# Interleaving two MLP blocks in thirds instead of halves: an attention, MLP and mixture-of-experts kernel on one core

## The chip, the cores and the metric

The kernel runs on one core of one Trainium2 chip. The metric is the device time of one execution in microseconds (us). The engines of a core are named as the profile names them: PE (TensorE, matmuls; PEld is its weight load), DVE (VectorE), ACT (ScalarE), POOL (GpSimd) and SP (SyncE, which here only issues DMAs).

## The reference

Three layers follow one another; the first two are what the change touches.

```python
def _attn_ref(q, k, v):                      # q, k, v: 4 batches x 8 heads x 576 x 64
    scores = scale * np.matmul(q, k.transpose(0, 1, 3, 2))
    mask_local = (rel >= 0) & (rel < stride)                 # heads 0-3, stride 32
    mask_strided = (rel >= 0) & (pos[None, :] % stride == pos[:, None] % stride)   # heads 4-7
    scores = np.where(masks[None, :, :, :], scores, -1000000000.0)
    ...                                      # softmax
    return np.matmul(attn, v)

def _moe_ref(x, w_gate, w_val, w_out):       # x: 2304 tokens x 512; FF = 1536
    g = x @ w_gate
    silu = g * (1.0 / (1.0 + np.exp(-g)))
    return (silu * (x @ w_val)) @ w_out

def _moe2_ref(x, ...):                       # 8 experts, each token goes to its two best
    ...                                      # router, then relu(x @ w1[e]) @ w2[e], weighted and summed
```

w_gate, w_val and w_out arrive as float64. q, k, v and the weights of the second mixture layer are float32.

## The kernel before, in words

**Tiling.** The 2304 tokens are six blocks (j = 0 to 5) of 384; the FF dimension of the MLP is twelve chunks (c = 0 to 11, `NC1`) of 128. One *chunk* below means one pair (j, c): `m_gate` (line 490) and `m_val` (line 498) make a 128x384 tile each from 12 matmuls, and `m_out` (line 513) adds the product into three PSUM banks of the block with 9 matmuls, one chunk later (`pend`). float32 operands are split into a high and a low half (`split`, line 402: a cast on ScalarE, a subtraction on VectorE or POOL), and three of the four products are taken (`PASSES`).

**VectorE's and ScalarE's part of a chunk.** ScalarE takes tanh of the gate (line 494); VectorE makes th (line 495), the product with the value tile (line 502) and its lower half (line 404, hhl); ScalarE makes the upper half (line 403). The gate and value tiles share two PSUM buffers (`ps_gv`), so the next gate's matmuls wait for line 495 or 502 of the chunk before.

**Weights.** Each 128-wide chunk of w_gate and of w_val is one *piece*. Its 512 KB of float64 are loaded into one of three `raw` buffers by a DMA on SP's queue (`load_weight`, line 408); `weight` (line 421) turns the float64 bit patterns into float32 with three VectorE operations (lines 427 to 429); `split` makes the halves, the lower one on POOL for chunk 1 and all later ones. The twelve finished chunks stay in SBUF (`W`). w_out is not kept: each chunk needs its own copy (`load_wo`, `split_wo`, lines 456 and 463). For block 0 it is loaded as float64, converted as above, split with POOL, and its float32 form written to the buffer wod in DRAM; later blocks load that, and VectorE makes the lower half.

**Attention.** It is a generator (line 354) of 56 *quads* (four heads by up to 128 queries): transposes of q and k, scores, softmax (VectorE lines 306 to 318, ScalarE line 309), transposes, product with v, all on the same engines. Its results land in `ring`. `NEED` (line 652) says how many quads each block needs: 11 for block 0, 22 for block 1, 28 for block 2, and so on.

**The order of the work around the change.** Before the MLP starts, eleven quads are done, and some matmuls on zeros keep the PE busy. Then `seq` (line 655) lists the chunks. Blocks 0 and 1 are interleaved in halves, since block 1 can use a weight chunk as soon as block 0 has used it: block 0 chunks 0 to 5, block 1 chunks 0 to 5, block 0 chunks 6 to 11, block 1 chunks 6 to 11. I call these four stretches of six chunks *runs*. Blocks 2 to 5 then follow whole. Each chunk has three `slot` calls (line 692) that advance attention towards `goal` (line 658) at a pace of 18 slots in a run of six chunks, and advance the routing of a finished block by one step. All of quads 11 to 21 stand in run 0; runs 1 and 2 have no attention (their goal is the same 22, and all six PSUM banks hold the two blocks' sums); run 3 has quads 22 to 27 and block 0's routing. At the end of each run the x halves of the next run's block are made (`split_x`, line 473; four operations on ScalarE and four on VectorE, five buffers).

In run 0 each chunk loads and makes the weights one or two chunks ahead (`load_wgv`, `split_wgv`). After run 0, `half_wgv` (line 449) makes one piece at a time and issues the load of the piece two further on; `MADE` (line 443) says how many pieces of the later chunks are made by the end of each step: with the entries below two pieces in the first step after run 0, two in the second, one in the third, and so on.

```python
MADE = (2, 4, 5, 7, 9, 10, 11, 12)
...
elif i - HC < len(MADE):
    for n in range(MADE[i - HC - 1] if i > HC else 0, MADE[i - HC]):
        half_wgv(HC + n // 2, n % 2)
```

The main loop is at line 817. `late_consts` (line 136: twelve small DMAs on SP's queue) is called at block 1's first chunk, `zero_dram` (line 146: 22 stores of zeros on SP's queue) at block 2's first. Which instruction stands where on an engine is decided when the program is built: a planner may set instructions that depend on nothing late ahead of others, so the order on an engine is not quite the order of the text.

Of the kernel before, what the change touches and what calls it, by code (L numbers as in the profile page):

```python
# [21 lines left out]
def attention_moe_kernel(ctx: ExitStack, tc: tile.TileContext, q, k, v, w_gate, w_val, w_out,  # L22
# [9 lines left out]
    NC1 = FF // P  # L32
# [11 lines left out]
    NBLK = NT // 384  # L44
# [387 lines left out]
    def load_wgv(c):  # L432
        for i, src in enumerate((w_gate, w_val)):
            load_weight(("gv", c, i), src[:, c * P:(c + 1) * P])

    def split_wgv(c):
        W[c] = wp.tile([P, 4, DM], F32R, name="W", tag="W")
        eng = nc.gpsimd if c >= 1 else None
        for i in range(2):
            split(W[c][:, 2 * i], W[c][:, 2 * i + 1], weight(("gv", c, i)), eng)  # L440


    MADE = (2, 4, 5, 7, 9, 10, 11, 12)

    def load_half(c, i):
        if c < NC1:
            load_weight(("gv", c, i), (w_gate, w_val)[i][:, c * P:(c + 1) * P])

    def half_wgv(c, i):
        if i == 0:  # L450
            W[c] = wp.tile([P, 4, DM], F32R, name="W", tag="W")
        x = weight(("gv", c, i))
        load_half(c + 1, i)
        split(W[c][:, 2 * i], W[c][:, 2 * i + 1], x, nc.gpsimd)
# [196 lines left out]

    NEED = [11, 22, 28, 39, 50, 56]

    HC = NC1 // 2
    seq = [(j, c) for h in range(2) for j in range(2) for c in range(h * HC, (h + 1) * HC)]
    seq += [(j, c) for j in range(2, NBLK) for c in range(NC1)]

    goal = [NEED[1], NEED[1], NEED[1], NEED[2]] + [NEED[min(j + 1, NBLK - 1)] for j in range(2, NBLK)]
    
    def part(i):  # L660
        return i // HC if i < 4 * HC else 2 + i // NC1

    warm = ps_gv.tile([P, DM], F32, name="warm", tag="gv")

# [27 lines left out]
    def slot(i):  # L692
        if early and had5[0] and not rts:
            next(early[0], None)
        if rts:
            if next(rts[0], "end") == "end":
                rts.pop(0)
        p = part(i)
        g0, pace = goal[p - 1] if p else NEED[0], 36 if p > 3 else 18
        nslot[0] += 1  # L700
        if goal[p] > g0:
            want = g0 + (goal[p] - g0) * min(nslot[0], pace) / pace
            while adone[0] < want - PB:
                if next(att, "end") == "end":
                    break
# [91 lines left out]
    def early_steps():  # L797
        load_info(0, 0, 4)
        load_info(1, 0, 4)
        for _ in range(EY[0]):  # L800
            yield
        info(0, 0)
        info(1, 0)
        for t in range(2):
            gather(0, t, EARLY)
            yield
        for _ in range(EY[1]):
            yield
        for t in range(4):
            xtrans(0, t)  # L810
            if t < 2:
                gather(0, t + 2, EARLY)
            for _ in range(3):
                yield

    EY = (3, 4, 2)
    for i, (j, c) in enumerate(seq):
        if j == NBLK - 1 and c == 0:
# [3 lines left out]
            early.append(early_steps())  # L822
        if i < HC:
            if c + 2 < HC:
                load_wgv(c + 2)
            if c + 1 < HC:
                split_wgv(c + 1)
            else:
                for n in range(2):
                    load_half(HC, n)  # L830
# [3 lines that stand above are left out]
# [8 lines left out]
        split_wo(i)  # L842
        m_gate(j, c)
        slot(i)
        m_val(j, c)
        if i + 1 < len(seq) and part(i + 1) > part(i):
            att_until(goal[part(i)])
            nslot[0] = 0
            for kk in KORD:
                split_x(seq[i + 1][0], kk)  # L850
        slot(i)
        if pend:
            pj, pc = pend.pop()
# [5 lines left out]
        if j == NBLK - 1 and c >= 1 and wnext[0] < E * NC2 and wnext[0] < 12:  # L859
            prep_w()  # L860
        slot(i)
        pend.append((j, c))

# [132 lines left out]
    with tc.If(worst > 0):  # L996
        for e in range(E):
            s0, nov = e * REG + CAP[e], (REG - CAP[e]) // P
            last = nc.values_load(ntile[0:1, e:e + 1], min_val=0, max_val=nov)
            with tc.For_i(0, last, 1) as t:  # L1000
# [17 lines left out]
                for c in range(NC2):  # L1018
# [8 lines left out]
                    h = ov.tile([P, P], F32, name="o_h")  # L1027
# [35 lines left out]
```

## Time and profile before

| | us |
|---|---|
| median of three runs | 1071.08 |
| lowest and highest | 1070.45, 1072.36 |
| profiled execution, its own time | 1072.54 |
| its span, first to last instruction | 1070.8 |
| chunks 0 to 5 (run 0), by the first gate matmul of each stretch | 64.4 |
| runs 1 and 2 (no attention) | 81.3 |
| run 3 | 52.2 |
| from the third block to the end of the span | 822.5 |

The profiled execution's time is 1.7 us more than its span, and 1.5 us more than the median of the three runs. Stretches are told in us from the start of the span. A busy time on VectorE includes time in which an instruction is held up by another engine's use of the memory.

### The profile page before, as it was taken

The numbers are of one execution on the slowest core, as the hardware profiler recorded it, in microseconds if no ns is written. First come the engines' busy times: TensorE is split into PE (matmuls) and PEld (weight loads), VectorE is DVE, ScalarE is ACT, GpSimd is POOL, SyncE is SP. The second block draws the span as 40 slices with busy tenths as digits, with TensorE's granted clock in tenths as the row PEclk, the third lists the DMA queues.
The fourth block names the chain that finished last, engine by engine and source line by source line (L and its number), as shares of the span: only waits on it lengthen the run. The fifth ranks groups of instructions, "written<-read, shape, count | busy, mean of one in ns | idle before, by whom it ended". The sixth has DMA issues, their size and how long they took to land. (4 is left out here: it accounts for less than half of the span.)

```text
span 1070.8 us, 17472 instructions
## 1 busy us (share of the span) xinstructions
PE 1032.2 (96%) x6262; PEld 896.1 (84%) x6268; DVE 582.1 (54%) x1528; ACT 443.5 (41%) x1107; POOL 374.9 (35%) x425
## 2 busy tenths in 40 slices
PE   7999999999999999999998989999999999999994
PEld 4677888878888888889988878999888888888884
DVE  6899897474565664453464625444545444544210
ACT  4776442454454554442453424343434333333211
POOL 6154333024031231020014527455545454545211
PEclk9999999999999999999999999999999999999997
DMA  8688465269362641221344607546554545453212
GB/s 184 152 218 201 132 185 167 67 191 199 94 78 64 137 51 55 77 63 41 99 148 96 211 1 148 119 102 156 128 126 126 128 110 141 107 146 68 36 21 30
DMA packets 186961, 123.26 MB, mean 115 GB/s; under 512 B 96224, under 2 KB 154080, under 8 KB 186864
## 3 DMA queue, kind: packets, MB, share of 16 engines
q1 hardware_dynamic: 168256, 92.23, 34.0%
q0 software_dynamic: 16016, 25.10, 12.7%
q10 hardware_dynamic: 2592, 4.72, 1.2%
q8 instruction: 51, 0.84, 0.3%
q14 instruction: 46, 0.38, 0.1%
HBM read 98.04 MB, written 23.91 MB: 114 GB/s over the span
## 5 line engine op out<-in xcount | busy, mean ns | idle before, releaser
L893 PE MATMUL acc<-W,hhl 128*128 128x512 f32 (+1 forms) x960 | 243.3, 393 | 2.8 <-DVE hhl L885 2.7
L881 PEld LDWEIGHTS ps_h<-xg,W 128*128 128x128 f32 x1536 | 229.4, 188 | 14.1 <-ACT xg L403 1.7
L881 PE MATMUL ps_h<-xg,W 128*128 128x256 f32 (+2 forms) x1536 | 239.8, 305 | 1.3 <-ACT xg L403 1.3
L893 PEld LDWEIGHTS acc<-W,hhl 128*128 128x128 f32 (+1 forms) x960 | 170.3, 184 | 36.4 <-DVE hhl L885 3.6
L751 POOL DMA_INDIRECT xrow<-x1d,idq x152 | 153.1, 1007 | 113.8 <-DVE xgT L540 57.1
L487 PE MATMUL ps_v<-xh,W 128*128 128x384 f32 x864 | 172.3, 344 | 3.3 <-DVE th L502 3.3
L487 PE MATMUL ps_g<-xh,W 128*128 128x384 f32 x864 | 169.3, 342 | 2.9 <-DVE th L495 2.4
L520 PE MATMUL acc<-wohl,hhl 128*128 128x512 f32 x648 | 169.3, 400 | 0.5 <-ACT hhl L403 0.4
L487 PEld LDWEIGHTS ps_g<-xh,W 128*128 128x128 f32 x864 | 150.2, 188 | 13.2 <-DVE th L495 4.8
L487 PEld LDWEIGHTS ps_v<-xh,W 128*128 128x128 f32 x864 | 151.5, 190 | 7.4 <-DVE th L502 3.9
L885 DVE SCALAR_TENSOR_TENSOR hhl<-ps_h,hhl 128x256 fp32r<-128x256 f32 (+2 forms) x128 | 60.2, 470 | 171.4 <-ACT hhl L884 171.4
L884 ACT ACTIVATE hhl<-ps_h 128x256 fp32r<-128x256 f32 (+2 forms) x128 | 54.7, 428 | 212.5 <-PE ps_h L881 212.4
L520 PEld LDWEIGHTS acc<-wohl,hhl 128*128 128x128 f32 x648 | 119.4, 189 | 25.2 <-issue 1.3
L404 DVE TENSOR_TENSOR W<-raw,W 128x512 fp32r<-128x512 f32 x128 | 83.8, 688 | 54.4 <-ACT W L403 52.7
L906 POOL DMA_INDIRECT out_dram<-y,ids x40 | 64.3, 1607 | 122.6 <-ACT y L905 113.1
L403 ACT CAST W<-raw 128x512 fp32r<-128x512 f32 x128 | 74.1, 618 | 64.9 <-PE acc L893 45.6
L633 POOL DMA_INDIRECT slotd<-payload,si x36 | 37.5, 1042 | 125.9 <-DVE si L620 88.4
L403 ACT CAST hhl<-th 128x384 fp32r<-128x384 f32 x72 | 36.9, 513 | 93.9 <-DVE th L502 93.8
L495 DVE SCALAR_TENSOR_TENSOR th<-th,ps_g 128x384 f32<-128x384 f32 x72 | 39.7, 551 | 57.4 <-ACT th L494 57.4
L232 POOL DMA_DIRECT2D v<-in_v_dram x28 | 19.4, 696 | 143.1 <-PE ps_o L337 129.0
L494 ACT ACTIVATE th<-ps_g 128x384 f32<-128x384 f32 x72 | 35.3, 490 | 77.0 <-PE ps_g L487 74.7
L309 ACT ACTIVATE sc<-sc,mn 126x126 f32<-126x126 f32 (+3 forms) x152 | 56.5, 374 | 20.5 <-DVE mn L306 20.1
(138 smaller groups left out, 1027.3 us busy)
## 6 DMA issues: line engine op xcount, KB each, us to landing
raw<-in_moe_w_dram SPq DMA_DIRECT2D x128, 256.0 KB
raw<-wod SPq DMA_DIRECT2D x60, 256.0 KB
raw<-in_moe_w_gate_dram SPq DMA_DIRECT2D x12, 512.0 KB
raw<-in_moe_w_val_dram SPq DMA_DIRECT2D x12, 512.0 KB
raw<-in_moe_w_out_dram SPq DMA_DIRECT2D x12, 512.0 KB
out_dram<-zero SPq DMA_DIRECT2D x20, 256.0 KB
x1d<-x ACTq DMA_DIRECT2D x15, 256.0 KB
xq<-x1d SPq DMA_DIRECT2D x60, 64.0 KB
```

What stands on the lines that cost most here:

```text
L309: nc.scalar.activation(s[:n, i, :m], s[:n, i, :m], AF.Exp, bias=mn[:n, i:i + 1], scale=-1.0, accum_out=rs[:n, i])
L403: nc.scalar.copy(dst_hi, src)
L404: (eng or nc.vector).tensor_tensor(dst_lo, src, dst_hi.bitcast(F32), op=OP.subtract)
L487: nc.tensor.matmul(ps, W[c][:, o + a, kk * P:(kk + 1) * P], XH[j, kk][:, b2, :], start=(kk == KORD[0] and a == 0 and b2 == 0), stop=(kk == ...
L495: nc.vector.scalar_tensor_tensor(t, t, 1.0, ps, op0=OP.add, op1=OP.mult)
L520: nc.tensor.matmul(ACC[j][t], h[:, a, t * P:(t + 1) * P], wo[:, b2, :], start=(c == 0 and a == 0 and b2 == 0), stop=(c == NC1 - 1 and a == 1))
L751: nc.gpsimd.indirect_dma_start(out=x[:, g, :], out_offset=None, in_=x1q[:4 * (PAD + rows), :], in_offset=bass.IndirectOffsetOnAxis(ap=IDQ[ ...
L881: nc.tensor.matmul(ps, w[:, a, kk * P:(kk + 1) * P], XG[e, g][:, kk, b2, :n], start=(kk == 0 and a == 0 and b2 == 0), stop=(kk == KD - 1 a ...
L884: nc.scalar.activation(h[:, 0, :n], ps, AF.Relu)
L885: nc.vector.scalar_tensor_tensor(h[:, 1, :n], ps, 0.0, h[:, 0, :n].bitcast(F32), op0=OP.max, op1=OP.subtract)
L893: nc.tensor.matmul(acc[:m], h[:, a, t * P:t * P + m], w[:, 2 + b2, :], start=(c == 0 and a == 0 and b2 == 0), stop=(c == NC2 - 1 and a == 1))
L906: s = nc.gpsimd.indirect_dma_start(out=out, out_offset=bass.IndirectOffsetOnAxis(ap=IDX[e, ti][:m], axis=0), in_=y[:m], in_offset=None, co ...
```

## The change

The first two blocks are interleaved in thirds: six runs of four chunks (block 0 chunks 0 to 3, block 1 chunks 0 to 3, block 0 chunks 4 to 7, block 1 chunks 4 to 7, block 0 chunks 8 to 11, block 1 chunks 8 to 11). Attention's eleven quads for block 1 now stand in the first run of four chunks (12 slots), the six for block 2 in the last (12 slots), and the four runs between them, sixteen chunks, have none. Sixteen pieces of w_gate and w_val (chunks 4 to 11) are made after run 0 instead of twelve (chunks 6 to 11); the new `MADE` has thirteen entries, and two of its steps make none. `split_x` is called at six boundaries instead of four.

```diff
-    MADE = (2, 4, 5, 7, 9, 10, 11, 12)
+    MADE = (2, 4, 5, 7, 8, 8, 9, 9, 11, 12, 13, 15, 16)
...
-    HC = NC1 // 2
-    seq = [(j, c) for h in range(2) for j in range(2) for c in range(h * HC, (h + 1) * HC)]
+    NH = 3
+    HC = NC1 // NH
+    seq = [(j, c) for h in range(NH) for j in range(2) for c in range(h * HC, (h + 1) * HC)]
     seq += [(j, c) for j in range(2, NBLK) for c in range(NC1)]
 
-    goal = [NEED[1], NEED[1], NEED[1], NEED[2]] + [NEED[min(j + 1, NBLK - 1)] for j in range(2, NBLK)]
+    goal = [NEED[1]] * (2 * NH - 1) + [NEED[2]] + [NEED[min(j + 1, NBLK - 1)] for j in range(2, NBLK)]
     
     def part(i):
-        return i // HC if i < 4 * HC else 2 + i // NC1
+        return i // HC if i < 2 * NC1 else 2 * NH - 2 + i // NC1
...
-        g0, pace = goal[p - 1] if p else NEED[0], 36 if p > 3 else 18
+        g0, pace = goal[p - 1] if p else NEED[0], 36 if p >= 2 * NH else 3 * HC
```

## Rows read from the trace of the kernel before

**Rows 1.** The page, part 1: busy us (share of the span) xinstructions.

```profile
PE 1032.2 (96%) x6262; PEld 896.1 (84%) x6268; DVE 582.1 (54%) x1528; ACT 443.5 (41%) x1107; POOL 374.9 (35%) x425
```

**Rows 2.** Windows: stretch, length, busy us (xinstructions) of each engine, PE clock, DMA share, GB/s.

```profile
50.50:114.90 64.40, 60.62 (x447) 49.66 (x448) 60.02 (x166) 41.71 (x143) 31.63 (x31) 1.00 0.82 201
114.90:154.40 39.50, 38.79 (x199) 34.97 (x197) 35.60 (x56) 16.16 (x34) 11.71 (x9) 1.00 0.51 149
154.40:178.40 24.00, 21.42 (x106) 18.56 (x107) 23.11 (x36) 6.62 (x14) 6.54 (x5) 1.00 0.64 218
178.40:196.20 17.80, 17.80 (x95) 16.57 (x94) 7.16 (x14) 6.71 (x13) 3.87 (x3) 1.00 0.05 15
196.20:248.30 52.10, 51.05 (x338) 42.85 (x337) 32.72 (x123) 26.59 (x78) 14.44 (x20) 0.97 0.61 172
```

**Rows 3.** Timeline of the PE, first gate matmuls of five chunks: start us, us, instruction.

```profile
50.47 1.71 PE L487 MATMUL ps_g<-xh,W 128*128 128x384 f32 x7
...
114.88 2.51 PE L487 MATMUL ps_g<-xh,W 128*128 128x384 f32 x12
...
189.85 2.28 PE L487 MATMUL ps_g<-xh,W 128*128 128x384 f32 x12
...
196.18 2.24 PE L487 MATMUL ps_g<-xh,W 128*128 128x384 f32 x12
...
248.33 2.25 PE L487 MATMUL ps_g<-xh,W 128*128 128x384 f32 x12
```

**Rows 4.** Waits of the PE, 50.5 to 248.3 us: us in total, times, longest.

```profile
PE ps_g L487 <- DVE th L495: 2.4, 5, 0.9
PE ps_p L324 <- DVE sc L318: 1.1, 1, 1.1
...
PE ps_s L292 <- ACT kT L267: 0.8, 1, 0.8
PE ps_s L303 <- ACT kT L267: 0.8, 1, 0.8
PE ps_g L487 <- DVE xh L404: 0.6, 2, 0.4
PE ps_t L254 <- ACT qT L267: 0.5, 1, 0.5
PE ps_t L254 <- ACT pt L326: 0.4, 1, 0.4
PE ps_v L487 <- DVE th L502: 0.4, 1, 0.4
PE ps_s L292 <- ACT pt L326: 0.2, 1, 0.2
```

**Rows 5.** Lines of VectorE by form, 50.5 to 114.9 us.

```profile
L428 DVE SCALAR_TENSOR_TENSOR xf<-raw,xf 128x512 int32<-128x512 int32 x16 | 14.8, 927 | 0.1
L429 DVE SCALAR_TENSOR_TENSOR xf<-raw,xf 128x512 int32<-128x512 int32 x16 | 12.9, 807 | 0.0
L427 DVE TENSOR_SCALAR xf<-raw 128x512 int32<-128x512 int32 x15 | 8.2, 547 | 1.5 <-DMA raw<-in_moe_w_gate_dram 1.5
...
L495 DVE SCALAR_TENSOR_TENSOR th<-th,ps_g 128x384 f32<-128x384 f32 x6 | 3.3, 545 | 0.6 <-ACT th L494 0.6
```

**Rows 6.** Lines of VectorE by form, 114.9 to 196.2 us.

```profile
L429 DVE SCALAR_TENSOR_TENSOR xf<-raw,xf 128x512 int32<-128x512 int32 x16 | 15.9, 1000 | 0.3
...
L404 DVE TENSOR_TENSOR xh<-ring,xh 128x384 fp32r<-128x384 f32 x11 | 7.9, 734 | 0.0
...
L404 DVE TENSOR_TENSOR wohl<-raw,wohl 128x512 fp32r<-128x512 f32 x6 | 4.1, 681 | 0.0
```

**Rows 7.** Timeline of the PE and window (columns of rows 2) in run 3.

```profile
232.29 0.70 PE L303 MATMUL ps_s<-kT,qT 64*126 64x126 f32 x6 [1.05 <-DVE d L626]
...
234.00:236.00 2.00, 2.00 (x9) 1.77 (x9) 1.38 (x11) 1.87 (x11) 0.00 (x0) 0.50 1.02 383
```

## The prediction, made before the changed kernel ran

> **What bounds the kernel now.** I read the page's engine totals first: the PE is busy 96% of the span and VectorE 54% [rows 1]. That average hides where the change acts, so I next took the busy time by stage. In chunks 0 to 5 (50.5 to 114.9 us) VectorE is busy 60.0 of 64.4 us; from 154.4 to 178.4 us it is busy 23.1 of 24.0 while the PE is busy only 21.4; right after, until 196.2 us, it is busy 7.2 of 17.8 and the PE has no gap at all [rows 2]. The reader should see an overload followed at once by slack. The PE's timeline gives the scale: a chunk without attention and without waits takes 196.18 - 189.85 = 6.33 us, run 0 takes 114.88 - 50.47 = 64.4, the two middle runs together 196.18 - 114.88 = 81.3, and the last short run 248.33 - 196.18 = 52.2 us [rows 3]. Twelve chunks at 6.33 are 76.0, so the middle runs hold **5.3 us too much**. The list of the PE's waits says what ends last there: 2.4 us for th (line 495), 0.6 for the lower half of xh, 0.4 for the product (line 502), all VectorE's [rows 4]; the rest of the 5.3 is the drain and refill around each wait. The other waits of that list, apart from one in the last short run that comes below, belong to attention in run 0: 1.1 + 0.8 + 0.8 + 0.5 + 0.4 + 0.2 = **3.8 us** [rows 4]. No row of the list names a DMA. What can be won is therefore small: 5.3 + 3.8 and the little in the last short run, about 1% of the time. Below, runs are counted from 0: four now (0 to 3), six after the change (0 to 5).
>
> **The change, part by part.** The matmuls are the same ones; only their order and the VectorE work between them move. The profiled execution took 1072.54 us, 1.46 above the median of 1071.08; I make the sum as a difference and take it off the median.
>
> *Run 0 becomes four chunks.* Two chunks leave: 64.4 - 2 x 6.33 = 51.7 us if waits stay. Does VectorE still fit? A piece of a float64 weight costs 0.927 + 0.807 + 0.547 = 2.28 us there [rows 5]. Sixteen pieces lie in this stretch (the x16 of line 428): six of w_out, ten of gate and value. With two chunks fewer, four of the ten and two of the six leave: 6 x 2.28 = 13.7. Two chunks also take away three MLP operations each, about 0.55 [rows 5]: 3.3. VectorE's 60.0 falls to 43.0 of 51.7 us, 83% instead of 93%. (Neighbouring records overlap a little, so the true figure is higher; if only four fifths come off, 46.4, still 90%.) Conversion gets no tighter. What does get tighter is attention: the same eleven quads stand in twelve slots instead of eighteen, and the MLP matmuls that cover them shrink from six chunks to four. If the 3.8 us of waits grow in the ratio 6/4 it is +1.9; if the looser VectorE ends the longest of them (1.1, for line 318) it is 1.1 less. I take **+0.8**, with ends 0 and +3.8 (waits doubled).
>
> *The runs without attention become sixteen chunks.* Today VectorE has 35.6 + 23.1 = 58.7 us of work until 178.4 [rows 2], where the PE by itself would need 63.5 - 5.3 = 58.2: the load is 101%. Then it idles. After the change this part has six pieces more than today's sixteen (line 429, x16 [rows 6]): four of gate and value that left run 0, and w_out for eight chunks of the first block instead of six. The work is 65.9 (35.6 + 23.1 + 7.2 [rows 2]) + 6 x 2.28 + 4 x 1.65 for the MLP operations + 2 x 0.68 for the lighter w_out halves + 8 x 0.73 for two more sets of x halves [rows 6] = 65.9 + 13.7 + 6.6 + 1.4 + 5.9 = 93.5 us, against 16 x 6.33 = 101.3: 92% throughout, with the last pieces made three steps before their use. By the new runs: run 1 has seven pieces, of which two will be made ahead in run 0 as two are today: 5 x 2.28 + 4 x (1.65 + 0.68 + 0.73) = 23.6 of 25.3; run 2 two pieces and four of w_out, 23.2; run 3 six, 25.9; run 4 one and four, 20.9. Only run 3 is over, by 0.6. To this I add the wait that a change of block costs when VectorE is full: 0.6 (both xh waits, one boundary [rows 4]), at the two boundaries behind runs 1 and 3, 1.2; behind runs 0, 2 and 4 VectorE has slack, as at the other boundaries now, which show no such wait. Left over: 0.6 + 1.2 = 1.8 of the 5.3, a gain of **3.5**. Ends: 5.3 (all gone), and 0 (the load bunches as it does now).
>
> *The last short run.* Six quads stand beside four chunks of the second block, with the first block's routing, where there were six chunks: 52.2 - 12.7 = 39.5 us. VectorE's 32.7 us [rows 2] loses two chunks of 2.3 and is 71% busy. Now one wait of 1.05 us stands here, for a VectorE queue in which routing's last operations are behind attention's transposes, and the clock is 0.50 at 234 to 236 us after it [rows 7]; over the stage it is 0.97 [rows 2], so 0.03 x 52.1 = 1.6 us. The pair may vanish (-2.7) or come twice (+2.7); with routing now ending a few slots later, beside the zero fill, I cannot say which, and take 0.
>
> *Costed at nothing.* Eight more casts of x on ScalarE, which is busy 29.5 of the 81.3 us [rows 2]; if that cover failed, each would be at most as long as its VectorE half, 0.73. The constants' DMAs on SP's queue move two chunks earlier and now stand nearer the raw weight loads; wod is read back four chunks after it is written instead of six, still 25 us; the wait on either would be the first DMA in the PE's list. The 22 zero stores keep their place at the third block's start. POOL makes as many lower halves as before, fewer of them in run 0.
>
> *The clock, from the other side.* With waits of up to 1.1 us in run 0 the granted clock stayed 1.00 there [rows 2, 4], the full 2.4 GHz; behind the 1.05 us wait in the last short run it fell to 0.50, the 1.2 GHz level [rows 7]. So a wait of that size does not decide it alone. The Trainium skill, "TensorE: Matmul & The Clock Gate", section "HAM oscillation — how this bites in real kernels", says that matmul bursts with idle gaps between them put the engine back to its slow clock again and again; by that rule a thinner run 0 would lose what the last short run loses, once or more. In run 0 the trace so far speaks against it, in the last short run for it.
>
> **Sum:** +0.8 - 3.5 + 0 = -2.7 us. 1071.1 - 2.7 = **1068.4 us**.
>
> **Rivals.**
> 1. *The overload only moves.* VectorE's order is fixed when the program is built, and not by the steps in which a piece is due: run 0's stretch already holds ten pieces of gate and value for the five chunks 2 to 6. If the planner again packs pieces ahead of th, the new runs 1 and 3 each carry an overload, the 3.5 is not won or is given back at the new boundaries, and the change does not do what it says. Time: 1071.1 + 0.8 - (0 to 2) = 1070 to 1072. For it: 92% is near enough to full that order decides. Against: today's waits come only where the load passes 100%.
> 2. *Attention becomes the bound of run 0* (slower). It decides from the point at which the PE waits for softmax operations and not they for the PE: eleven quads in 51.7 us, 4.7 each against 5.9 now, with scores, exponentials and copies behind weight conversions on VectorE and ScalarE. Price: waits doubled (+3.8) and the two boundaries unrelieved (3.5 - 1.2 = 2.3 won): +1.5; with one clock drop in run 0 and one more in the last short run, 1.6 each: +4.7. Time 1072.6 to 1075.8, say 1074.5. For it: each of the six waits of run 0 is of that kind. Against: VectorE's share falls there.
> 3. *Everything fits.* The 5.3 goes, and the last short run's wait with its clock drop too: 1071.1 - 5.3 - 2.7 + 0.8 = 1063.9.
>
> **How the numbers follow.** A measurement of this kernel can tell 0.2%, 2.1 us, from no change. The forecast (1066.5 to 1069.5) has 0.35, rival 3 (1062.5 to 1066.5) 0.12, rival 1 0.27, rival 2 0.26. Faster by over 0.2% (below 1068.9) takes all of rival 3 and most of the forecast: 0.44. Within: rest of the forecast, rival 1 and the edge of rival 2: 0.30. Slower: 0.26. The range that leaves a tenth on each side is 1064 to 1075; the forecast's own is 1066.5 to 1069.5.
>
> **What would show it.** Right: in the changed profile, chunks 0 to 3 take 51.5 to 54 us, the sixteen chunks after them 102 to 104 us, the PE's waits for th in them fall under 1 us in total, and VectorE has no stretch of 20 us at 96% followed by one at 40%. The last four chunks of the pair take 37 to 42 us. Wrong: run 0 above 56 us or a granted clock under 1.00 there (rival 2); th waits of 2 us or more, now at the ends of runs 1 and 3 (rival 1); a DMA in the PE's list of waits; or a difference that arises after the third block begins, where the sum has nothing.

## The result, and the profile after

| | before | after |
|---|---|---|
| median (us) | 1072.3 (6 runs) | 1090.05 (6 runs) |
| lowest, highest | 1070.45, 1078.17 | 1078.21, 1090.58 |
| ratio, 95% interval | | 1.014 (1.0116 to 1.0164) |
| span of the profiled execution | 1070.8 | 1088.7 |

The changed kernel is 1.4% slower; the forecast was 1068.4, its range ended at 1075. The executions are of two kinds: four took 1089.7 to 1090.6 us at a mean granted clock of 0.977 to 0.980, two took 1078.2 and 1081.5 at 0.989 and 0.987; the profiled one (1090.4) is of the first kind, and the first section of the loss below is what sets the two apart.

The first reading is where the 17.9 us arise. The windows of the changed kernel (stretch, length, busy us of PE, PEld, DVE, ACT, POOL, PE clock, DMA share, GB/s), first by the stretches of the forecast, then inside run 0:

```profile
50.10:110.90 60.80, 59.31 (x383) 46.35 (x382) 42.49 (x146) 38.20 (x135) 23.27 (x25) 0.80 0.62 151
110.90:221.80 110.90, 105.33 (x529) 94.42 (x528) 87.02 (x141) 40.48 (x80) 31.80 (x22) 0.98 0.48 141
221.80:254.60 32.80, 32.80 (x227) 26.95 (x226) 19.31 (x47) 13.31 (x37) 6.24 (x10) 1.00 0.47 108
254.60:369.50 114.90, 109.69 (x717) 92.49 (x716) 64.41 (x255) 54.21 (x168) 31.19 (x41) 0.97 0.58 129
...
62.00:64.00 2.00, 0.66 (x3) 0.48 (x3) 2.00 (x4) 1.24 (x3) 0.95 (x1) 1.00 0.32 49
64.00:66.00 2.00, 2.00 (x13) 1.44 (x12) 2.00 (x11) 1.08 (x4) 0.72 (x2) 0.88 0.81 256
66.00:88.00 22.00, 22.00 (x93) 15.67 (x92) 10.46 (x54) 11.59 (x48) 7.05 (x10) 0.50 0.46 107
```

The same 22 us in the kernel before:

```profile
66.00:88.00 22.00, 22.00 (x155) 17.80 (x156) 20.62 (x69) 15.96 (x60) 13.88 (x16) 1.00 0.86 201
```

Run 0 takes 60.8 us where two chunks less than before would be 51.7 [rows 2, 3]: **+9.1**. VectorE has slack, busy 42.5 of 60.8; from 64 us on the PE is busy all the time, but at **half its clock** from 66 to 88 us, and it gets through 93 matmuls there where the kernel before has 155. The sixteen chunks without attention take 110.9, against 106.6 for before's twelve plus four at 6.33: **+4.3**. From the last short run to the third block's first finished sums (line 531, at 369.5 us) it is 32.8 + 114.9 = 147.7; before took 349.7 - 196.2 = 153.5 with two chunks more, so 140.8: **+6.9**. Together 20.3; two or so are won back by the end of the span. In the last of these stretches the four chunks of the last run took only 32.8 us, and the third block 114.9 where it had taken 101.4: 18 of the 24 score matmuls of line 303 that stood in the last run before, and the end of the routing, now run in the third block. The rest of this section takes the three sites in turn.

The PE's waits of the changed kernel (us in total, times, longest), by the same three stretches, to be laid beside [rows 4]:

```profile
PE ps_s L303 <- ACT kT L267: 1.5, 1, 1.5
...
PE ps_g L487 <- DVE xh L404: 3.3, 5, 0.9
PE ps_g L487 <- DVE th L495: 2.0, 2, 1.4
...
PE acc L520 <- ACT wohl L403: 2.2, 1, 2.2
PE ps_r L607 <- DVE cm L603: 1.8, 1, 1.8
PE ps_s L292 <- DVE cm L603: 0.6, 1, 0.6
PE ps_s L303 <- DVE oh L618: 0.6, 1, 0.6
```

In run 0 one wait of 1.5 us is left of the six that made 3.8 before. The other two stretches got new ones: xh 3.3 instead of 0.6, and routing (cm, oh) and w_out halves (wohl), where the kernel before had 1.1 us for another routing value (d, [rows 7]) and 0.5 us for cm. The PE's timeline shows where they stand (start, duration, instruction; in brackets the idle time before and what ended it):

```profile
63.34 0.48 PE L303 MATMUL ps_s<-kT,qT 64*126 64x126 f32 x2 [1.48 <-ACT kT L267]
...
137.44 0.79 PE L487 MATMUL ps_g<-xh,W 128*128 128x384 f32 x3 [0.50 <-DVE xh L404]
138.98 1.14 PE L487 MATMUL ps_g<-xh,W 128*128 128x384 f32 x5 [0.75 <-DVE xh L404]
165.04 1.86 PE L487 MATMUL ps_g<-xh,W 128*128 128x384 f32 x7 [1.39 <-DVE th L495]
...
196.81 2.02 PE L487 MATMUL ps_g<-xh,W 128*128 128x384 f32 x8 [0.92 <-DVE xh L404]
...
270.17 0.18 PE L607 MATMUL ps_r<-cm,ones 128*128 128x32 bf16 x1 [1.81 <-DVE cm L603]
271.63 4.21 PE L487 MATMUL ps_g<-xh,W 128*128 128x384 f32 x12
288.62 0.96 PE L520 MATMUL acc<-wohl,hhl 128*128 128x512 f32 x3 [2.19 <-ACT wohl L403]
```

*Run 0.* The wait at 62 us is behind a copy of transposed k by ScalarE. The timelines of ScalarE, VectorE and POOL in the changed kernel:

```profile
62.36 0.62 ACT L403 CAST wohl<-xf 128x512 fp32r<-128x512 f32 x1 [2.00 <-DVE xf L429]
62.88 0.71 ACT L267 COPY kT<-ps_t 128x288 f32<-128x288 f32 x2
...
58.82 0.41 DVE L427 TENSOR_SCALAR xf<-raw 128x512 int32<-128x512 int32 x1
60.23 1.50 DVE L427 TENSOR_SCALAR xf<-raw 128x512 int32<-128x512 int32 x1
61.65 0.68 DVE L429 SCALAR_TENSOR_TENSOR xf<-raw,xf 128x512 int32<-128x512 int32 x1
...
60.05 1.40 POOL L404 TENSOR_TENSOR W<-xf,W 128x512 fp32r<-128x512 f32 x1 [2.77 <-ACT W L403]
```

Read from the bottom: POOL's subtraction from 60.05 us stretches VectorE's line 427 from 0.41 to 1.50 us; line 429 of the w_out piece ends at 62.3; ScalarE's cast of that piece has stood idle 2.00 us for it, with the kT copies behind it in the queue; the PE needs them. The kernel before has the same chain; there it is line 429 itself that the subtraction stretches:

```profile
60.44 1.79 DVE L429 SCALAR_TENSOR_TENSOR xf<-raw,xf 128x512 int32<-128x512 int32 x1
...
63.25 0.48 PE L303 MATMUL ps_s<-kT,qT 64*126 64x126 f32 x2 [0.75 <-ACT kT L267]
```

Its kT copies start at 62.79 us, in the changed kernel at 62.88, which is nearly the same. What differs is that the PE of the changed kernel has done its earlier matmuls at 61.86 us and not at 62.50, so it waits 1.48 us instead of 0.75. The stretched operation is part of the wait in both kernels; it is not what made it longer. Behind the wait the clock stayed at 1.00 before, and here it falls to 0.50. On VectorE's stretched operation the Trainium skill, "GPSIMD Engine Reference", section "1. Specifications", says that POOL's way to SBUF is shared with VectorE; the trace agrees, 1.50 against 0.41 us.

*The sixteen chunks.* Chunks of 6.2 to 6.6 us everywhere except at three of the changes of block: chunk 8 (counted from 0 through the whole order) takes 8.0, chunks 11 and 12 8.1 and 9.75, chunks 15 and 16 7.4 and 8.0. Over 6.33 each that is 1.7 + 5.2 + 2.8 = 9.7, all of the stretch's 110.9 - 101.3 = 9.6. (Of the 5.2 at the middle one some 1.5, by estimate, is clock: it is at 0.50 there from 168 to 171 us, and half of these 3 us is lost.) VectorE's timeline at the middle one, and the DMA issues on SP's queue there and at the third block's start, in the changed kernel:

```profile
159.36 0.56 DVE L404 TENSOR_TENSOR hhl<-th,hhl 128x384 fp32r<-128x384 f32 x1
164.09 0.43 DVE L427 TENSOR_SCALAR xf<-raw 128x512 int32<-128x512 int32 x1 [4.18 <-DMA raw<-in_moe_w_out_dram]
164.44 0.55 DVE L495 SCALAR_TENSOR_TENSOR th<-th,ps_g 128x384 f32<-128x384 f32 x1
...
159.41 0.33 SPq L416 DMA_DIRECT2D raw<-in_moe_w_out_dram  x1
...
253.69 25.53 SPq L152 DMA_DIRECT2D out_dram<-zero  x20
281.22 0.33 SPq L416 DMA_DIRECT2D raw<-wod  x1
```

The w_out load is issued at 159.41 and lands at 164.09, VectorE stands 4.18 us before its line 427, and th, which the PE is waiting for (the 1.39 above), is the next instruction in VectorE's queue. The PE's list of waits names th; the cause is a DMA. The waits of VectorE over the sixteen chunks, and of SP's queue from 157 to 160 us, in the changed kernel:

```profile
DVE xf L427 <- DMA raw<-in_moe_w_out_dram: 6.7, 2, 4.2
DVE xf L427 <- DMA raw<-in_moe_w_gate_dram: 0.8, 1, 0.8
...
SPq L416 <- DVE xf L429: 2.8, 1, 2.8
```

VectorE waits 7.5 us for weight loads here; in the two middle runs of the kernel before it waits for none. The load at 159.41 was not issued earlier because its raw buffer was still being read: SP's queue had waited 2.8 us for a line 429, the last operation to read one.

*The end of the pair.* The twenty zero stores occupy SP's queue from 253.69 to 279.2 us, that is, during the first chunks of the third block, and the w_out loads of that block stand behind them: the 2.19 us wait for wohl at 288.62. In the kernel before the same view reads:

```profile
231.95 15.02 SPq L152 DMA_DIRECT2D out_dram<-zero  x20
```

They were done at 247.0, before the third block began at 248.33 [rows 3]. In the changed kernel SP's queue had waited 5.5 us for the tile of zeros that the stores read, which VectorE writes (line 148). Why their issue then took 25.5 us instead of 15.0 no run shows. The routing of the first block also moved: its last steps now end the PE's waits at 268 to 271 us, and the gate of twelve matmuls that follows takes 4.21 us instead of 2.25, at half clock once more (0.50 from 270.5 to 277 us).

### The profile page after: what moved, and what is told of

It is laid out like the page before. It is cut to its first block, busy times and chain, and to the rows that moved or that the text cites. A ratio compares the mean times of both kernels' runs of the same rounds, so it can differ in the third digit from the quotient of the medians.

```text
span 1088.7 us, 17488 instructions
## 1 busy us (share of the span) xinstructions
PE 1049.2 (96%) x6262; PEld 907.7 (83%) x6268; DVE 581.7 (53%) x1536; ACT 446.4 (41%) x1115; POOL 376.3 (35%) x425
## 5 line engine op out<-in xcount | busy, mean ns | idle before, releaser
L487 PE MATMUL ps_g<-xh,W 128*128 128x384 f32 x864 | 177.6, 349 | 5.5 <-DVE xh L404 3.3
L520 PE MATMUL acc<-wohl,hhl 128*128 128x512 f32 x648 | 173.3, 405 | 2.4 <-ACT wohl L403 2.2
L487 PEld LDWEIGHTS ps_g<-xh,W 128*128 128x128 f32 x864 | 153.7, 192 | 18.0 <-DVE xh L404 6.1
```

The source lines that it names most:

```text
L487: nc.tensor.matmul(ps, W[c][:, o + a, kk * P:(kk + 1) * P], XH[j, kk][:, b2, :], start=(kk == KORD[0] and a == 0 and b2 == 0), stop=(kk == ...
L520: nc.tensor.matmul(ACC[j][t], h[:, a, t * P:(t + 1) * P], wo[:, b2, :], start=(c == 0 and a == 0 and b2 == 0), stop=(c == NC1 - 1 and a == 1))
```

## The experiments

In their kernels the sizes of the runs are a list: (6, 6) is the kernel before, (4, 4, 4) the change. Ratios are to the kernel before on the same chip, whose median is 1070 to 1072 us, but 1081 on the chip of four_two_six, route_late, warm0 and halves_spread. First the stretches of the kernels with thirds, in us, by the first gate matmul of chunks 0, 4 and 20 and the third block's first line 531; the first line is the kernel before, brought to the same number of chunks at 6.33 us each. A line is read from one profile; the two profiles of the changed kernel differ by 2.6 us in the last stretch, so smaller differences show little. On the slower chip most of the extra 10 us lies behind these stretches (726.6 to 729.0 us from block 2's sums to the end, 717.5 to 722.4 on the others), but the kernel before was not profiled there.

| kernel | run 0 | sixteen chunks | then to block 2's sums | sum |
|---|---|---|---|---|
| before | 51.7 | 106.6 | 140.8 | 299.2 |
| after | 60.8 | 110.9 | 147.7 | 319.4 |
| thirds_again | 60.7 | 110.8 | 150.3 | 321.8 |
| jit | 63.7 | 109.8 | 147.9 | 321.4 |
| warm0 | 59.8 | 109.3 | 149.6 | 318.7 |
| zero_late | 51.2 | 111.5 | 144.1 | 306.8 |
| route_late | 50.5 | 110.7 | 144.0 | 305.2 |
| late_both | 50.5 | 110.4 | 139.2 | 300.1 |
| free_bounds | 57.8 | 108.2 | 149.8 | 315.8 |
| k_on_dve | 50.7 | 109.9 | 149.9 | 310.5 |
| all_three | 51.5 | 107.4 | 139.1 | 298.0 |

### The order alone: short_first and short_last

```diff
-    SIZES = (4, 4, 4)
+    SIZES = (4, 8)     # short_first, MADE = (2, 4, 6, 8, 9, 11, 12, 13, 14, 15, 16)
+    SIZES = (8, 4)     # short_last, MADE = (1, 2, 3, 4, 5, 6, 7, 8)
```

> First run of four chunks, then eight (sizes 4, 8): the attention of run 0 is squeezed as in thirds, the last short run has eight chunks. Theory A (three separate sites: the half clock of run 0 costs about 9 us, DMA waits in the middle 4, the pile-up behind the last short run 7): run 0 takes 59 to 62 us with a stretch of over 15 us at a granted clock of 0.50, the end is near the kernel before; total 1078 to 1084, and 11 less in an execution in which the clock holds. Rival B (thirds are slow because there are more boundaries, everywhere): only one more short run than before, run 0 about 52 us, total 1071 to 1074.

> First run of eight chunks, last of four (sizes 8, 4): only the end is squeezed. Theory A: the granted clock holds in run 0, no long DMA wait in the middle, but the attention and routing of the last short run run over into the third block, with the zero stores ahead of the weight reads on the queue: 1075 to 1079. Rival B: 1071 to 1073. Rival C (all of the loss is run 0's clock): 1068 to 1071.

short_first: 1069.84 us, ratio 1.0026 (0.9991 to 1.0061). short_last: 1087.05, ratio 1.0164 (1.0142 to 1.0186). The profiled short_first has the thirds' run 0, with the same wait, and another clock. Its windows and the row of the PE's timeline:

```profile
62.00:64.00 2.00, 0.57 (x4) 0.29 (x2) 2.00 (x4) 0.95 (x3) 0.39 (x2) 1.00 0.30 105
64.00:88.00 24.00, 23.83 (x167) 18.61 (x168) 20.87 (x77) 18.75 (x69) 12.32 (x15) 1.00 0.81 198
```

```profile
64.03 0.48 PE L303 MATMUL ps_s<-kT,qT 64*126 64x126 f32 x2 [1.46 <-ACT kT L267]
```

A wait of 1.46 us, then full clock, and run 0 in 50.5 us. So a short run 0 with eleven quads is not slow in itself, and the wait does not decide alone. Two of its ten executions had a mean clock of 0.978 and 0.980 and took 1082.8 and 1081.3 us; the others 1068.7 to 1074.3. short_last keeps a longer first run and a last run of four chunks. From the last run to block 2's sums it takes 148.1 us, as the thirds do, so the short last run costs by itself. Its eight-chunk first run takes 90.0 us, 12.9 more than before's six with two at 6.33: it had new waits for kT of 2.4 and 2.2 us with the clock at 0.50 behind them (73.5 to 83.7 and 114.5 to 121.3 us); so it is no clean test of run 0, and its time is above all three ranges that had been expected. Between the two stand its twelve chunks without attention, at 6.30 us each, and the PE waits for nothing in them:

```profile
140.60:216.20 75.60, 75.60 (x397) 70.70 (x396) 47.70 (x86) 27.01 (x52) 13.14 (x10) 1.00 0.37 114
```

Eight pieces are left to make there, one a chunk, and VectorE is busy 47.7 of 75.6 us. The 5.3 us that the prediction wanted to win are won in this stretch, behind a first run that loses more.

### Weights and the clock: jit, warm0

```diff
-        load_half(c + 1, i)                          # jit, in half_wgv
...
+            for n in range(MADE[i - HC], (MADE + MADE[-1:])[i - HC + 1]):
+                load_half(HC + n // 2, n % 2)        # jit: gate and value pieces loaded one step before they are made
...
+                        nc.tensor.matmul(x.rearrange("p a b -> p (a b)"), wz[:, :P], wz[:, :2 * P], start=True, stop=True)   # warm0
```

> Thirds, but a piece's raw load is issued one step before the piece is made, not when the piece two before it is made, so that in the steps that make none the raw buffers are free for w_out. Theory A: the 4.18 us in which VectorE waits for the raw w_out near 164 us goes, and with it the PE's waits and the lower clock behind it; the sixteen chunks without attention take 105 to 108 us instead of 110.9; total 3 to 6 us under thirds in an execution with the same clock in run 0. Rival: the DMA is late because of the DMA engines' load and not for want of a buffer: 110 to 112 us there, total as thirds.

> Thirds, with matmuls on zeros (results never read) in run 0: twelve of 256 columns ahead of the scores of the second batch's first quad, where the PE waits 1.5 us, and two of 512 columns ahead of the probability transposes of five quads; no other work changes. Theory A (the half clock from 66 to 89 us follows that wait and the thin matmul work behind it): the granted clock is 1.00 through run 0 in the profile, run 0 takes 51 to 55 us, and executions lie at 1077 to 1084 with none near 1090. Rival (the clock falls for another reason, or independent of the PE's work): still 1088 to 1092 in most executions.

jit: 1092.89 us, ratio 1.0217 (1.0195 to 1.0239). The wait for the w_out DMA is gone, but VectorE now waits 2.4 and 3.2 us for gate and value pieces, and the PE 4.9 us for th: the sixteen chunks stay at 109.8. The wait moved from one load to the others; whether weights loaded further ahead would end it is not shown. warm0 issues extra matmuls on zeros in run 0 whose results are never read: 1098.47 us, ratio 1.0152 (1.0125 to 1.0178). The half clock shrank to about 72 to 79 us. But ten of the twelve matmuls set ahead of the scores stand behind the wait for kT, which is still 1.6 us, and the PE then waits 2.2 us for mn, a VectorE operation of the softmax. So the wait was not filled, and the run does not tell whether filling it would hold the clock.

### The end of the pair: zero_late, route_late, late_both

```diff
-            if (j, c) == (2, 0):
+            if (j, c) == (2, 4):                 # zero_late, late_both: zero_dram
...
-                rts.append(routing(pj))
+                held.append(routing(pj))         # route_late, late_both
+                if pj:
+                    rts.extend(held)
+                    held.clear()
```

> Thirds, with the 22 zero stores called at the fifth chunk of the third block instead of its first. Theory A: the PE's wait of 2.2 us for the w_out half in the third block's second chunk goes, the stretch from the end of the sixteen chunks to the end of the third block's sums is 141 to 145 us instead of 147.7, total 3 to 6 us under thirds at the same clock in run 0. Rival: the pile-up is attention and routing in too few slots, and the queue only a bystander: 146 to 148 us, total as thirds.

> Thirds, with the first block's routing held back until the second block's is due, so that the last run of four has attention alone. Theory A (attention and routing of the last short run stand in each other's way): the PE's waits for routing operations (2.4 us) and the lower clock behind them go; from the end of the sixteen chunks to block 2's sums 136 to 140 us instead of 142 to 148; total 3 to 6 under thirds at the same clock in run 0. Rival: the wait moves to a later place of the third block, and the total stays within 1.5 us.

> Thirds with both late edits: the zero stores at the third block's fifth chunk, and the first block's routing held back until the second block's is due. Theory A (both stand in the way of the last short run): from the end of the sixteen chunks to block 2's sums 138 to 142 us, where the kernel before by the same count has 140.9 and thirds 147.7; total 5 to 8 under thirds at the same clock in run 0. Rival (the loss is attention in twelve slots): 143 to 146 us as with either edit alone.

zero_late: 1084.05 us, ratio 1.0112 (1.0075 to 1.0148); the last stretch is 144.1 and no wait for wohl is left, the routing waits are. route_late: 1098.57, ratio 1.0171 (1.0147 to 1.0194); the stretch is 144.0. One routing wait stands at a later place (cm 1.5), beside 1.5 us for th and 2.0 us with no cause in the profile, and the wait for wohl is gone here too. For this edit moved the zero stores as well, although their call stands where it did:

```profile
235.61 15.14 SPq L152 DMA_DIRECT2D out_dram<-zero  x20
```

They end 2.3 us into the third block, which begins at 248.5, and not 25 us into it. So route_late is no test of the routing alone. late_both: 1081.17, ratio 1.0063 (1.0025 to 1.01); 139.2, and of the PE's waits in that stretch one remains:

```profile
PE ps_g L487 <- DVE th L495: 1.4, 1, 1.4
```

Each edit is worth 3.6 to 6.3 us against the two unaltered kernels' 147.7 and 150.3, and both together 8.5 to 11.1. The third site is these two, and with both the last stretch is 1.6 us under the kernel before; some of this is clock, which in the profiles is 0.50 for 7 us of the changed kernel's stretch and never below 1.00 in late_both's. How the loss divides between stores and routing is not shown, since route_late relieves both. That the zero stores were costed at nothing was wrong.

### The sixteen chunks: four_two_six, halves_spread, free_bounds

```diff
-    SIZES = (4, 4, 4)
+    SIZES = (4, 2, 6)      # four_two_six
...
-    MADE = (2, 4, 5, 7, 9, 10, 11, 12)
+    MADE = (1, 2, 3, 4, 5, 7, 8, 9, 10, 11, 12)      # halves_spread: the kernel before, pieces spread
...
-    MADE = (2, 4, 5, 7, 8, 8, 9, 9, 11, 12, 13, 15, 16)
+    MADE = (2, 4, 6, 6, 6, 8, 10, 10, 10, 12, 14, 14, 14, 15, 16)      # free_bounds
```

> Six runs as in thirds and the same list of pieces, but of 4, 2 and 6 chunks: as many changes of block as thirds, the same run 0, and a last run of six chunks as before. Theory A (the last short run of four is what costs in an execution with the full clock): block 2's sums end 4 to 7 us earlier relative to the sixteen chunks than in thirds, total 1070 to 1075 with the full clock in run 0, 10 to 12 more without. Rival B (the changes of block cost): as thirds, 1077 to 1081 with the full clock.

> The kernel before with its two runs of six, and only the list of pieces changed: twelve pieces over eleven steps, one a step, instead of over eight. Theory A (pieces packed ahead of th cause the 5.3 us of waits in the middle runs): the middle runs take 77 to 79 us instead of 81.3, total 1067 to 1069. Rival (the planner packs as it can, whatever the list says, or the wait moves): 80 to 82 us, 1069 to 1072.

> Thirds, and only the list of pieces changed: none is made in the chunks on either side of a change of block, two in the steps between. Theory A (a change of block costs because x's lower halves stand behind conversions on VectorE): the chunks on either side of a change come down from 7.4 to 9.7 us to 6.5 to 7.5, the sixteen chunks from 110.9 to 103 to 107 us, total 4 to 8 under thirds at the same clock. Rival (w_out's conversions and loads, which stay, are what is in the way): 109 to 112 us.

halves_spread: 1082.76 us, ratio 1.0011 (0.9979 to 1.0043). Its two middle runs take 82.6 us, before's 81.3: its waits are th 3.1 and xh 0.7 us, where before had 2.4 and 0.6 [rows 4]. Spreading the pieces by itself wins nothing. The conversions do spread, over ten chunks instead of eight, but VectorE now waits 10.0 us for weight loads in these runs, where it waited for none:

```profile
DVE xf L427 <- DMA raw<-in_moe_w_out_dram: 4.6, 3, 1.9
DVE xf L427 <- DMA raw<-in_moe_w_val_dram: 3.1, 2, 2.7
DVE xf L427 <- DMA raw<-in_moe_w_gate_dram: 2.3, 2, 1.7
```

One wait was exchanged for another. four_two_six: 1091.31, ratio 1.0105 (1.0067 to 1.0142), its fourteen chunks without attention 99.0 us, 10.4 over 14 x 6.33, again at the changes of block (8.1, 10.7, 8.5, 8.1 us), with 3.5 us of waits for xh and 2.1 for th. Its last run has six chunks, as before, and takes 157.1 us to block 2's sums where before takes 153.5, with the clock at 0.98 in the mean and on the slower chip; so a run of six has lost less there than the 6.9 of the run of four, but not nothing. free_bounds makes no piece in the steps around a change: 1091.07, ratio 1.0127 (1.0043 to 1.0212). All waits for xh and th are gone, the changes at chunks 8 and 16 cost nothing; what is left stands at chunks 10 to 12, in the PE's waits:

```profile
PE acc L520 <- POOL wohl L404: 2.5, 3, 1.0
PE acc L520 <- ACT wohl L403: 1.8, 2, 1.1
```

So the queue of VectorE was the cost at two changes and w_out was at the third, where this list of pieces did not help (VectorE waits 6.4 us for w_out's loads in these sixteen chunks): 108.2 instead of 110.8, only 2.6 won.

### Repeat, and run 0: thirds_again, k_on_dve

```diff
-                    (nc.vector.tensor_copy if nm == "k" and b == 0 else nc.scalar.copy)(dst, ps)
+                    (nc.vector.tensor_copy if nm == "k" else nc.scalar.copy)(dst, ps)      # k_on_dve
```

> The changed kernel again, unaltered, as the reference for the other three on the same chip. Theory A: executions fall into two groups by the mean granted clock of the core, about 0.978 and about 0.988, some 11 us apart, because the half clock of run 0 is chance; a profile of the second group shows run 0 at 50 to 52 us and the same waits everywhere else. Rival (the half clock belongs to the kernel's order): one group.

> Thirds, with the second batch's transposed k copied by VectorE instead of ScalarE, so that the copy does not stand behind w_out's cast on ScalarE, which itself waits for VectorE. Theory A (the half clock of run 0 needs the PE's wait of 1.5 us at 62 us): the wait falls under 0.8 us, the clock stays at 1.00 in run 0, executions 1076 to 1082 on the first chip's scale, that is no group 11 us above. Rival (the thin PE work from 66 to 89 us is enough by itself): two groups as in thirds.

thirds_again, the changed kernel unaltered: 1083.2, 1089.8, 1094.0 and 1096.4 us at clocks of 0.990, 0.980, 0.975 and 0.974, ratio 1.0144 (1.0067 to 1.0222), the half clock in run 0 again. k_on_dve: 1085.06 (1080.9 to 1086.4, 9 runs), ratio 1.0104 (1.0075 to 1.0133), one kind of execution only, clocks of 0.984 to 0.990. Its window where the changed kernel ran at half clock:

```profile
62.00:88.00 26.00, 25.79 (x184) 20.09 (x183) 23.16 (x83) 18.02 (x67) 13.11 (x15) 1.00 0.79 186
```

The waits for ScalarE's kT are gone (a 1.2 us wait for VectorE's copy stands at 60 us instead), run 0 takes 50.7 us and costs VectorE 2.5 us more than the 42.5 of the changed kernel, where it has room.

### All three sites, and candidates: all_three, before_k, short_first_k, short_first_all

all_three is k_on_dve, free_bounds and late_both together; before_k is the kernel before with the line of k_on_dve; the last two are short_first with that line, and with late_both's edits too.

> Thirds with all three sites relieved at once: k copied by VectorE (run 0), pieces kept away from the changes of block (the sixteen chunks), zero stores and the first block's routing later (the end of the pair and the third block). If the account by three separate sites is whole, the pieces add up: run 0 50.5 to 51.5 us at a granted clock of 1.00, the sixteen chunks 104 to 107, from there to the third block's sums 142.5 to 144.5, the time 1.000 to 1.006 of the kernel before, in one group of executions with a mean clock of 0.985 or more. If the sites share one resource and a relief at one only moves the loss to the next (rival), the time stays at 1.007 to 1.013, as with each relief alone, with new waits on VectorE or ScalarE in one of the three stretches.

> The kernel before (halves) with the second batch's transposed k copied by VectorE. If the rare long executions of the kernel before (about 1080, mean clock 0.978 to 0.983) are the same half clock behind the same wait for ScalarE's copy of k, none is left: all executions at a mean clock of 0.985 or more, the median 0.998 to 1.002 of the kernel before. If they come from elsewhere (rival), one execution in five stays near 1.01. If VectorE, busy 60.0 of 64.4 us in run 0, cannot take the copies, run 0 grows from 64.4 to 66 or more and the ratio is 1.002 to 1.005.

> Runs of four and eight chunks (one change of block fewer in the interleaving than thirds have, none more than halves), with k copied by VectorE. If its long executions are the half clock behind the wait for ScalarE's copy of k, they go: all at a mean clock of 0.985 or more, the median 0.997 to 1.001 of the kernel before. If another wait can start the half clock (rival), some stay near 1.010.

> As the run with four and eight chunks and k copied by VectorE, with the zero stores and the first block's routing later. If the late loss of the thirds comes of their last run having only four chunks, there is little to win here with eight: within 1 us of the run without the two delays, 0.996 to 1.001 of the kernel before. If the zero stores and the routing cost the same here as in the thirds (rival), 3 to 6 us less: 0.992 to 0.996.

all_three: 1073.23 us (1070.4 to 1074.7, 12 runs), clocks 0.988 to 0.995, beside 1072.35 (1068.6 to 1081.2, 35 runs) of the kernel before; ratio 0.9982 (0.9957 to 1.0007). The loss of 1.4% is gone. Its windows by stretch, to be laid beside those of the changed kernel, and its waits in the sixteen chunks:

```profile
51.00:102.50 51.50, 49.26 (x382) 38.68 (x383) 45.77 (x153) 34.47 (x126) 22.59 (x25) 1.00 0.74 179
102.50:209.90 107.40, 104.35 (x530) 95.04 (x529) 86.31 (x141) 42.14 (x81) 34.99 (x23) 0.98 0.49 146
209.90:349.00 139.10, 137.56 (x942) 116.39 (x941) 82.24 (x300) 67.92 (x205) 36.37 (x51) 1.00 0.55 131
```

```profile
PE acc L520 <- POOL wohl L404: 1.9, 2, 1.0
PE acc L520 <- ACT wohl L403: 1.1, 1, 1.1
```

The stretches give back 9.3, 3.5 and 8.6: 21.4 us. The first is inside its expectation, the second 0.4 above it, the third 3.4 under it (the expectation had taken one chunk's start in late_both too early; by the timeline its stretch is 139.2, not 143.5). The three sites do not feed on one another, and together they are the whole loss: with all three relieved nothing of it is left. Nothing is won over the kernel before that a measurement can tell.

before_k: 1077.71, ratio 1.0035 (1.0012 to 1.0059). Run 0 grows to 69.0 us, by 4.6:

```profile
50.20:119.20 69.00, 62.49 (x447) 50.80 (x447) 64.36 (x175) 40.03 (x136) 33.63 (x31) 0.98 0.76 188
```

VectorE, busy 60.0 of 64.4 us there [rows 2], cannot take the copies: the expectation's third case. An estimate of 1.7 of the 4.6 us is clock, half of the 3.4 us at the lower level: behind a wait of 2.1 us for qT it is 0.51 from 95.9 to 99.3 us. short_first_k: 1072.35 (1071.0 to 1073.7), ratio 0.9983 (0.9961 to 1.0004), the steadiest of all. short_first_all: 1074.31, ratio 1.0005 (0.9983 to 1.0028); its last stretch is 163.7 us against 162.7 without the two delays. With eight chunks in the last run the two delays win nothing: what they relieve belongs to the short last run.

## Why the prediction was wrong, step by step

The measured time lies beyond the range and beyond every rival's, the longest of which was 1075.8. The two executions at the higher clock, 1078.2 and 1081.5 us, lie beyond it too, so no single step explains the miss; three terms of the sum failed.

**Run 0, taken as +0.8, was +9.1.** The work was sized well: VectorE's 43.0 us was 42.5, and the waits did not grow from 3.8 to 4.6, they fell to 1.5. At full clock the step is a gain, 50.5 to 51.5 against 51.7. What failed is the paragraph on the clock: from a clock of 1.00 behind waits of up to 1.1 us it took that the drop was unlikely, and where rival 2 allowed one it was priced at 1.6 us, the size it has in the last short run [rows 7]. Measured, the level stays at 0.50 for 24 us (65.5 to 89.4): the engine then works through matmuls without a gap but at half speed. Run 0 is the longer, the longer this lasts: 57.8 us with 17 us at 0.50 (free_bounds), 60.8 and 60.7 with 24 (the changed kernel, twice), 63.7 with 31 (jit), and 50.5 to 51.5 with none. Of ten executions of the changed kernel seven have a mean clock of 0.980 or less; in the six of the first table the two kinds lie 10.5 us apart, about what run 0 loses in the profile.

Whether it falls is not decided by the wait alone: the same wait (1.43 to 1.51 us) is followed by 0.50 in the profiles of the changed kernel, thirds_again, free_bounds and jit, and by 1.00 in those of short_first, zero_late, route_late, late_both and four_two_six. But where the wait for ScalarE's kT is taken away, the long fall does not come: of 21 executions of the two kernels with thirds and k on VectorE none had a mean clock under 0.984, against the 7 of 10 at 0.980 or less; with runs of four and eight it is none of 24 against 2 of 10. That is what the runs show of the cause.

For the kernel before the same is likely and not shown: 7 of its 35 executions beside before_k lie under 0.984 and none of before_k's 12, but no such execution was profiled. Nor is this wait the only one that can start a fall, as before_k shows with a short one. The Trainium skill, "TensorE: Matmul & The Clock Gate", section "HAM oscillation — how this bites in real kernels", was quoted for a thinner run 0 that loses clock by idle gaps coming again and again. The trace agrees that the clock falls behind an idle gap of the PE, 1.48 us here; it does not show gaps again and again, for the PE has none from 64 to 88 us while the clock stays at 0.50. No run here shows what tips it, though every fall in run 0 stands behind a wait.

**The sixteen chunks, taken as -3.5, were +4.3.** The premise was that the 5.3 us of today are an overload of 101%, ended by spreading the pieces to 92%. halves_spread did the spreading without the thirds and won nothing: VectorE was then less busy, and stood waiting for weight loads. In the thirds the load was even lower than worked out, 87.0 us and not 93.5, and yet the PE's waits are 5.3 us. With less work the premise holds: short_last, with VectorE busy 63% of its twelve chunks, has no wait in them. At the 87.0 of 110.9 us of the thirds two things were left out. One is order: at a change of block, th of the old block, the x halves of the new one and the pieces stand in one queue, and the PE needs the first two at once (free_bounds, which keeps the pieces away, has no such wait left). The other is the loads: VectorE's waits for weights, 7.5 us of them, have no term in the sum. The step "0.6 at a change of block, at two boundaries" is the mis-sized term: it was 1.7, 5.2 and 2.8 at three. Rival 1 had the mechanism (a packed queue at the new changes of block) and let the stretch win 0 to 2 us; it lost 4.3. The 5.2 has a DMA in it, the w_out load that VectorE waits 4.18 us for; that a late load would show as a DMA in the PE's list was wrong, the list names what stands behind it.

**The last short run, taken as 0, and "the zero stores keep their place", costed at nothing: +6.9.** The stores kept their place in the text and not in time: before they ended 1.4 us ahead of the third block, now they run 25 us into it. late_both shows that the stores and the routing together are this loss, short_first_all that with a longer last run delaying them wins nothing. The sign that the last four chunks take 37 to 42 us failed on the other side: they took 32.8, because work that should have stood beside them ran on into the third block.

**Rival 2** pointed to the right side and the right run, with a wrong mechanism (attention was not the bound: its waits fell) and a clock drop priced at a seventh of what it costs. Of the signs that the prediction named, "run 0 above 56 us or a granted clock under 1.00 there" and "a difference that arises after the third block begins" both came; of the th waits of rival 1 there are 2.0 us in all, 1.39 of it behind the DMA.

What stays open: why the clock falls in some executions of one and the same program and not in others, and how much of the 6.1 us left in all_three's sixteen chunks is w_out, for which no run had more raw buffers.

## What to carry to other kernels

Price a clock drop by how long the level can last in the stretch where it may fall, not by the shortest drop that the trace shows, and look at several executions' mean clocks before believing that a wait is harmless. Cost a move by the queues that it shifts: stores that are issued "at the start of" a block are free only while they end before it, and what stands behind them decides. A load of 92% spread evenly says nothing of a place where three consumers meet in one queue; count the instructions between two waits there, and ask whether the loads that they read can be in time.

## What the runs showed of the hardware that was not expected

Half clock can last 17 to 31 us although the PE has no gap in it: 93 matmul records at clock 0.50 from 66 to 88 us, where the kernel before has 155 in the same time at 1.00. By the mean clock one program falls into it in seven executions of ten; both that were profiled show it. The same wait of 1.4 to 1.5 us is followed by it in four profiles and by full clock in five. And beside a subtraction on POOL an operation of VectorE took 1.50 us instead of 0.41, or 1.79 instead of 0.68, with a cast on ScalarE and then the PE waiting behind it.
